# A chunked recurrence on 64x64 array tiles: wider moving operands, fewer calls, and the next chunk's systems woven into the current one

## The chip, the cores and the metric

The kernel runs on one core of a Trainium2 chip. The metric is device time in microseconds. The core's engines run their own queues side by side: TensorE (PE, matmuls and weight loads), VectorE (DVE), ScalarE (ACT), GpSimd (POOL) and SyncE (SP, whose queue issues most DMAs). They wait for one another by semaphores.

## The reference

Two blocks follow each other. The first is a linear recurrence (RWKV-7) over 768 steps, for 4 batches of 8 heads of size 40, with a 40x40 state for each:

```
y[t]  = r[t] @ state
Sa    = state @ a[t]
state = state * w[t] - outer(Sa, b[t]) + outer(v[t], k[t])
```

Its output is brought to 3072 rows of 320. The second block is a mixture of 8 experts: logits `x @ w_gate`, the best expert of each row, its softmax weight, then `relu(x @ w1[e]) @ w2[e]` (320 to 1024 to 320) times that weight, for the rows of each expert. All is in float32.

## The kernel before, in words

**The recurrence** is done in 12 chunks of 64 steps (NS). 32 sequences (batch x head) are held as two units s, each of 16 sequences: two batches with four pairs of heads make eight groups g, and the two heads of a pair (par) stand in the partitions 0 to 63 and 64 to 127. The list HD runs over the 16 pairs (g, par), so nearly every step of a unit is 16 small matmuls, one for each sequence. `eh` picks the own half of the partitions, `dh` the other one, and `qd` a quarter of 32.

Within a chunk, `decay` makes running products of w by a scan (L247), their reciprocals (L254), and scales k, a and b by them on POOL (L257). `natural` turns k, v and b from (feature, step) to (step, feature) by a matmul with a unit matrix. `gram` makes the 64x64 Gram matrices GT (k with a) and AT (v with r), masked on POOL (L296). `invert` inverts the 64x64 unit-triangular matrix of a with b: `inv_n` makes the two 32x32 diagonal blocks N and the block below them, `inv_sq` squares N four times, `inv_tt` builds the product of (I + N^k), all on 32x32 tiles of the PE array (`quads`: 32 matmuls for a unit), and `inv_w` and `inv_f` couple the two halves. `right` makes the right sides q from the state and from GT with v; `solve` multiplies by the inverse F, once as u and once turned as uT; `zgram` makes ZT; `state` the next state; `turned` its transpose; `y_state` and `y_rest` the output y; `emit` turns y to rows, adds the logits and writes rows to DRAM (x_rows).

**The order.** On PE the order is the one that is written out (`manual_schedule`); `turns` takes two calls at a time from each of its lists. In chunk c the written order is: loads of chunk c + 2 (`load_kab`), right sides with natural k and b of chunk c + 1, y from the state with GT of c + 1 and the solve, zgram with state, decay of c + 2, the rest of y with AT and natural v of c + 1, loads of v and r of c + 2, emit, and then the whole inversion for chunk c + 1, with nothing beside it but the two units' turns. On the other engines and on SP's queue a planner sets the order, by the written order and by what it takes to be ready. Buffers: kab has three for each unit, wp two, and PSUM has six banks for results of one bank and one pair of banks for y and emit.

**After the recurrence** come the routing (counts and places of the rows, in vector operations) and the experts: gathers of rows by indirect DMA, `turn`, `layer1` (L769), `layer2` (L782), and a scatter (L788). All matmuls of the recurrence are recorded under one line, L208, that of the helper `mm`; they are told apart by their tiles.

Of the kernel before, what the change touches and what calls it, by code (L numbers as in the profile page):

```python
# [8 lines left out]
F32 = mybir.dt.float32  # L9
# [12 lines left out]
def kernel(  # L22
# [16 lines left out]
    nc = tc.nc  # L39
# [79 lines left out]
    with tc.tile_pool(name="ring", bufs=1) as ring, \  # L119
         tc.tile_pool(name="sb", bufs=2) as sb, \  # L120
# [11 lines left out]
        def eh(par, n=D):  # L132
            return slice(par * 64, par * 64 + n)

        def dh(par, n=D):
            return slice((1 - par) * 64, (1 - par) * 64 + n)

        def qd(par, i):
            q = 2 * (1 - par) + i
            return slice(q * 32, q * 32 + 32)  # L140

        kab_r = [[ring.tile([128, 2, 3, NP, T2], F32, name=f"kab{s}_{i}") for i in range(3)] for s in range(NB2)]
        wp_r = [[ring.tile([128, G, T2 + 1], F32, name=f"wp{s}_{i}") for i in range(2)] for s in range(NB2)]
        x_r = [ring.tile([128, G, 64], F32, name=f"xt{s}") for s in range(NB2)]
        for tl in kab_r:
            for t in tl:
                for lo in (32, 96):
                    nc.gpsimd.memset(t[lo : lo + 32], 0.0)
        for tl in wp_r:
            for t in tl:  # L150
                for lo in (32, 96):
                    nc.gpsimd.memset(t[lo : lo + 32], 1.0)
                nc.gpsimd.memset(t[:, :, 0:1], 0.0)
# [3 lines left out]


        def padded(name, n):
            ts = [ring.tile([128, G, 64], F32, name=f"{name}{i}") for i in range(n)]  # L160
            for t in ts:
                nc.gpsimd.memset(t[:, :, D:], 0.0)
            return ts

        nk_r = [padded(f"nK{s}_", 2) for s in range(NB2)]
        st_r = [padded(f"ST{s}_", 2) for s in range(NB2)]
        s_r = [padded(f"S{s}_", 2) for s in range(NB2)]
        q_r = padded("q", NB2)


        i32 = ring.tile([128, 32], F32, name="i32")
        low32 = ring.tile([128, 32], F32, name="low32")
        for q in range(4):
            qs = slice(q * 32, q * 32 + 32)
            nc.gpsimd.tensor_copy(i32[qs], ident[qs, qs])
            nc.gpsimd.tensor_scalar(low32[qs], after[qs, qs], scalar1=-1.0, scalar2=None, op0=ALU.mult)
        up64 = ring.tile([128, T2], F32, name="up64")
        for q in range(2):
            qs = slice(q * 64, q * 64 + 64)
            nc.gpsimd.tensor_copy(up64[qs], before[qs, qs])  # L180
        for t in x_r:
            nc.gpsimd.memset(t[:], 0.0)
            for q in (0, 2):
                qs = slice(q * 32, q * 32 + 32)
                nc.gpsimd.tensor_copy(t[qs, :, 0:32], i32[qs, None, :].to_broadcast([32, G, 32]))
        iw = ring.tile([128, NP, D + E], F32, name="iw")
        for par in range(2):
            nc.gpsimd.tensor_copy(
                iw[eh(par), :, :D], ident[eh(par), None, par * 64 : par * 64 + D].to_broadcast([D, NP, D]),
            )  # L190
            nc.sync.dma_start(
                iw[eh(par), :, D:], moe_w_gate.rearrange("(p a e) x -> a e p x", p=NP, a=2)[par],
            )

        def bank(name, w=T2):
            return pp.tile([128, G, w], F32, name=name, tag="ps", bufs=6)

        def turns(*lists):

            lists = [list(l) for l in lists if l]  # L200
            while any(lists):
                for l in lists:
                    for _ in range(2):
                        if l:
                            l.pop(0)()
# [4 lines left out]
        units, wide = {}, {}  # L210

        def src(u, b2):
            c, s = u
            return c * T2 // C, c * T2 % C, 2 * s + b2

        def load_kab(u):
            c, s = u
            d = units[u] = {"kab": kab_r[s][c % 3], "wp": wp_r[s][c % 2]}
            for b2 in range(2):
                ch, o, b = src(u, b2)  # L220
                for par in range(2):
                    nc.sync.dma_start(
                        d["wp"][eh(par), b2 * NP : b2 * NP + NP, 1:], packed[b, ch, par, :, W, :, o : o + T2],
                    )
                for par in range(2):
                    nc.sync.dma_start(d["kab"][eh(par), b2], packed[b, ch, par, :, K : B_ + 1, :, o : o + T2])

        def load_vr(u):
            c, s = u
            d = units[u]  # L230
            d["vr"] = sb.tile([128, 2, 2, NP, T2], F32, name=f"vr{s}")
            for b2 in range(2):
                ch, o, b = src(u, b2)
                for par in range(2):
                    nc.sync.dma_start(d["vr"][dh(par), b2], packed[b, ch, par, :, V : R + 1, :, o : o + T2])

        def kab(d, n, g):
            return d["kab"][:, g // NP, n, g % NP, :]

        def vr(d, n, g):  # L240
            return d["vr"][:, g // NP, n, g % NP, :]

        def decay(u):
# [7 lines left out]
            wi = sb.tile([128, 2, NP, T2], F32, name="wi")  # L251
            P4 = PT[:].rearrange("q (b p) t -> q b p t", b=2)
            for h in range(2):
                nc.vector.reciprocal(wi[:, h], P4[:, h, :, 1:])  # L254
            k = d["kab"]
            for n, m in ((0, wi[:]), (1, P4[:, :, :, :T2]), (2, wi[:])):
                nc.gpsimd.tensor_tensor(k[:, :, n], k[:, :, n], m, op=ALU.mult)  # L257

        def natural(u, nm):

            c, s = u
            d = units[u]
            ps = bank("ps_nat", D)
            ts = []
            for g, par in HD:
                if nm == "V":
                    x, h, at = vr(d, 0, g), dh(par), (1 - par) * 64
                else:
                    x, h, at = kab(d, 0 if nm == "K" else 2, g), eh(par), par * 64
                ts.append(lambda x=x, h=h, at=at, g=g, par=par: mm(ps[eh(par, 64), g, :], x[h], ident[h, at : at + D]))  # L270

            def end():
                if nm == "K":
                    t = d["nK"] = nk_r[s][c % 2]
                else:
                    t = d["n" + nm] = sb.tile([128, G, D], F32, name=f"n{nm}{s}")
                nc.scalar.copy(t[:, :, :D], ps[:])
            return ts, end

        def gram(u, nm):  # L280
# [3 lines left out]
            ps = bank("ps_" + nm)  # L284
            ts = []
            for g, par in HD:
                if nm == "GT":
                    l, r, h = kab(d, 0, g), kab(d, 1, g), eh(par)
                else:
                    l, r, h = vr(d, 0, g), vr(d, 1, g), dh(par)  # L290
                ts.append(lambda l=l, r=r, h=h, g=g, par=par: mm(ps[eh(par, 64), g, :], l[h], r[h]))

            def end():
                t = d[nm] = sb.tile([128, G, T2], F32, name=f"{nm}{s}")
                nc.scalar.copy(t[:], ps[:])  # L295
                nc.gpsimd.tensor_tensor(t[:], t[:], up64[:, None, :].to_broadcast([128, G, T2]), op=ALU.mult)  # L296
# [4 lines left out]
        def quads(f):  # L301
            for g in range(G):
                for i in range(2):
                    for par in range(2):
                        f(g, par, i)

        def inv_n(u):
            c, s = u
            d = units[u]
            ps = bank("ps_N")  # L310

            def one(g, par, i):
                a, b = kab(d, 1, g), kab(d, 2, g)
                h = eh(par)
                if i == 0:
                    mm(ps[qd(par, 0), g, 32:], a[h, :32], b[h, :32])
                else:
                    mm(ps[qd(par, 1), g, :], a[h, 32:], b[h, :])
            quads(one)
            N = d["N"] = sb.tile([128, G, 32], F32, name=f"N{s}", bufs=3)  # L320
            nc.vector.tensor_tensor(N[:], ps[:, :, 32:], low32[:, None, :].to_broadcast([128, G, 32]), op=ALU.mult)
            NT = d["NT"] = sb.tile([128, G, 32], F32, name=f"NT{s}", bufs=3)
            nc.vector.transpose(NT[:].rearrange("q g t -> q (g t)"), N[:].rearrange("q g t -> q (g t)"))
            n21 = d["n21"] = sb.tile([128, G, 32], F32, name=f"n21{s}", bufs=1)
            for q in (1, 3):
                qs = slice(q * 32, q * 32 + 32)
                nc.scalar.activation(n21[qs], ps[qs, :, :32], AF.Copy, scale=-1.0)
# [537 lines left out]
```

## Time and profile before

| | |
|---|---|
| median of 3 runs | 1310.56 us (1308.91 to 1318.55) |
| the profiled execution | 1320.06 us |
| its span, first to last instruction | 1318.3 us |
| mean granted TensorE clock | 0.749 of full speed |
| PE busy / weight loads busy | 947.3 us / 735.6 us |
| DVE / ACT / POOL busy | 337.6 / 222.8 / 286.3 us |
| matmul instructions | 30652, and as many weight loads |

The profile is one execution. Busy times are unions over an engine's instructions, so a matmul's own duration (its pipeline included) is longer than the distance between two of them. "Issue" is time in which an engine waited for nothing that the profile shows. The granted clock is 1.00 for 2.4 GHz and 0.50 for 1.2 GHz.

### The profile page before, as it was taken

Reading aid. Unit: us, or ns where it says so; the run is one execution under the profiler, and the core shown is the slowest. Engines: PE = TensorE matmul, PEld = TensorE weight load, DVE = VectorE, ACT = ScalarE, POOL = GpSimd, SP = SyncE. Lnnn points to the kernel's source line nnn. Section 1 sums busy time; section 2 is a strip of 40 time slices with the busy share of each in tenths; the row PEclk is TensorE's granted clock in tenths of the full one; section 3 lists DMA queues with packets and bytes.
Section 4 is the critical chain, followed back from the end, with each engine's and each line's share of the span. In section 5 each row is a group of like instructions: output and inputs, shape, how many; then the busy total and the mean of one; then the engine's idle time right before and its main releaser. Section 6 shows DMA issues by size and latency. Waiting matters only on the chain.

```text
span 1318.3 us, 64132 instructions
## 1 busy us (share of the span) xinstructions
PE 947.3 (72%) x30652; PEld 735.6 (56%) x30652; DVE 337.6 (26%) x627; ACT 222.8 (17%) x496; POOL 286.3 (22%) x302
## 2 busy tenths in 40 slices
PE   0656575857568575866757475756479999999996
PEld 0556575746567575766757475656325544554454
DVE  1542333151514214051514212031511110111100
ACT  0212121212212121211212121211001111111110
POOL 9813231030403113030403101010132012211011
PEclk9998575665756576575757566575779999999998
DMA  3402021201102020111102010000533132322100
GB/s 67 106 4 63 11 59 29 56 22 36 43 13 52 18 59 19 36 43 31 37 5 59 9 29 9 9 10 9 130 101 114 55 100 76 115 75 89 47 15 16
DMA packets 116827, 61.86 MB, mean 47 GB/s; under 512 B 100945, under 2 KB 112211, under 8 KB 116564
## 3 DMA queue, kind: packets, MB, share of 16 engines
q1 hardware_dynamic: 110356, 48.52, 14.3%
q0 software_dynamic: 3072, 9.20, 2.3%
q8 instruction: 241, 3.95, 1.3%
q10 hardware_dynamic: 3136, 0.01, 0.1%
q14 instruction: 22, 0.18, 0.0%
HBM read 49.83 MB, written 9.19 MB: 45 GB/s over the span
## 4 chain that ended last, share of the span: by engine, by line
issue 43%; PE 39%; POOL 9%; DVE 5%; DMA 1%; SPq 1%; ACT 0%; POOLq 0%; ACTq 0%; DVEq 0%
PE ps_tt L208 7%; PE ps_sq L208 7%; PE ps_nat L208 4%; PE ps_f L208 3%; PE ps_y L208 3%; PE ps_q L208 3%; DVE wi L254 3%; POOL out_dram L788 2%; PE ps_s L208 2%; POOL xg L750 2%; PE ps_w L208 2%; PE ps_u L208 1%; POOL kab L257 1%; PE ps_GT L208 1%; DVE PT L247 1%
## 5 line engine op out<-in xcount | busy, mean ns | idle before, releaser
L769 PE MATMUL hp<-xgT,w 128*128 128x512 f32 (+1 forms) x384 | 192.0, 630 | 0.0
L208 PE MATMUL ps_tt<-TT,N 32*32 32x32 f32 x6144 | 105.8, 236 | 88.5 <-issue 84.4
L208 PE MATMUL ps_sq<-N,NT 32*32 32x32 f32 x6144 | 104.6, 236 | 87.9 <-issue 73.3
L208 PEld LDWEIGHTS ps_tt<-TT,N 32*32 32x32 f32 x6144 | 94.9, 151 | 95.3 <-issue 90.7
L208 PEld LDWEIGHTS ps_sq<-N,NT 32*32 32x32 f32 x6144 | 94.5, 151 | 95.6 <-issue 95.5
L782 PE MATMUL zp<-w,h_sb 128*128 128x320 f32 x512 | 145.0, 433 | 0.0
L769 PEld LDWEIGHTS hp<-xgT,w 128*128 128x128 f32 (+1 forms) x384 | 63.3, 189 | 123.3 <-issue 122.2
L296 POOL TENSOR_TENSOR GT<-GT,up 128x512 f32<-128x512 f32 x24 | 30.5, 1271 | 447.5 <-ACT GT L295 447.5
L208 PE MATMUL ps_nat<-ident,kab 40*64 40x40 f32 x1536 | 85.1, 295 | 44.8 <-POOL kab L257 41.8
L782 PEld LDWEIGHTS zp<-w,h_sb 128*128 128x128 f32 x512 | 94.6, 191 | 34.5 <-issue 0.8
L208 PEld LDWEIGHTS ps_nat<-ident,kab 40*64 40x64 f32 x1536 | 81.4, 212 | 46.6 <-POOL kab L257 41.8
L788 POOL DMA_INDIRECT out_dram<-zo,s_idx x32 | 31.8, 995 | 278.4 <-ACT zo L787 278.4
L774 DVE TENSOR_SCALAR h_sb<-hp 128x512 f32<-128x512 f32 x32 | 22.2, 692 | 247.1 <-PE hp L769 244.4
L254 DVE RECIPROCAL wi<-PT 128x256 f32<-128x256 f32 x48 | 82.1, 1733 | 5.3 <-POOL kab L257 3.9
L350 DVE TENSOR_TENSOR TT<-ps_tt,TT 128x256 f32<-128x256 f32 x96 | 40.8, 425 | 161.2 <-PE ps_tt L208 158.8
L338 ACT COPY N<-ps_sq 128x256 f32<-128x256 f32 x96 | 35.7, 372 | 263.5 <-PE ps_sq L208 260.6
L257 POOL TENSOR_TENSOR kab<-kab,wi 128x512 f32<-128x512 f32 x48 | 65.7, 1381 | 33.3 <-DVE wi L254 33.3
L445 DVE TENSOR_TENSOR ZT<-ps_z,up 128x512 f32<-128x512 f32 x24 | 16.6, 690 | 197.1 <-PE ps_z L208 197.1
L296 POOL TENSOR_TENSOR AT<-AT,up 128x512 f32<-128x512 f32 x24 | 41.9, 1747 | 108.5 <-ACT AT L295 108.5
L341 DVE STREAM_TRANSPOSE NT<-N 128x256 f32<-128x256 f32 x72 | 32.0, 444 | 100.1 <-ACT N L338 100.0
L776 ACT ACTIVATE h_sb<-hp 128x512 f32<-128x512 f32 x32 | 19.1, 597 | 202.9 <-PE hp L769 202.9
L208 PE MATMUL ps_f<-xt,i 32*32 32x64 f32 x768 | 45.5, 305 | 7.4 <-issue 7.4
(168 smaller groups left out, 1771.5 us busy)
## 6 DMA issues: line engine op xcount, KB each, us to landing
kab<-in_packed_dram SPq DMA_DIRECT2D x96, 120.0 KB
w<-in_moe_w_dram SPq DMA_DIRECT2D x8, 1280.0 KB
w<-in_moe_w_dram SPq DMA_DIRECT2D x8, 1024.0 KB
vr<-in_packed_dram SPq DMA_DIRECT2D x96, 80.0 KB
wp<-in_packed_dram SPq DMA_DIRECT2D x96, 40.0 KB
x_rows<-xr SPq DMA_DIRECT2D x48, 80.0 KB
w<-in_moe_w_dram SPq DMA_DIRECT2D x8, 256.0 KB
xg<-x_rows,g_idx POOLq DMA_INDIRECT x32
```

The source lines that it names most:

```text
L208: nc.tensor.matmul(out_, lhsT=lhs, rhs=rhs, start=start, stop=stop, skip_group_check=free)
L254: nc.vector.reciprocal(wi[:, h], P4[:, h, :, 1:])
L257: nc.gpsimd.tensor_tensor(k[:, :, n], k[:, :, n], m, op=ALU.mult)
L296: nc.gpsimd.tensor_tensor(t[:], t[:], up64[:, None, :].to_broadcast([128, G, T2]), op=ALU.mult)
L338: nc.scalar.copy(N[:], ps[:])
L341: nc.vector.transpose(NT[:].rearrange("q g t -> q (g t)"), N[:].rearrange("q g t -> q (g t)"))
L350: nc.vector.tensor_tensor(TTn[:], ps[:], TT[:], op=ALU.add)
L750: nc.gpsimd.indirect_dma_start(out=g["xg"][:, j, :], out_offset=None, in_=x_d[:, :], in_offset=bass.IndirectOffsetOnAxis(ap=g["gi"](j), ax ...
L769: nc.tensor.matmul(hp[:, :cols], lhsT=g["w"][0][:dsz, db, fb * 128 : (fb + 1) * 128], rhs=g["xT"][:dsz, db, :cols], start=(db == 0), stop= ...
L774: nc.vector.tensor_relu(g["h"][:, fb, :cols], hp[:, :cols])
L782: nc.tensor.matmul(zp[:], lhsT=g["h"][:, fb, j * 128 : (j + 1) * 128], rhs=g["w"][1][:, fb, :], start=(fb == 0), stop=(fb == FB - 1),)
L788: ins_ = nc.gpsimd.indirect_dma_start(out=out[:, :], out_offset=bass.IndirectOffsetOnAxis(ap=g["si"](j), axis=0), in_=zo[:], in_offset=Non ...
```

## The change

All matmuls of the recurrence use 64x64 tiles. The moving operand of a matmul is widened where two products share the stationary one. Tiles `ai` and `ri` hold a and r (64 columns) with a 40x40 unit matrix behind them, so that one matmul of 104 columns gives a Gram matrix and the turned operand: `gtk` gives GT and natural k, `atv` gives AT and natural v, `ntb` gives the system and natural b, and `zgram` gives ZT and u (so `solve` makes only uT). A tile `pair` holds the power N^k beside the inverse so far, so that one matmul of 128 columns squares and multiplies (`level`). The two 32x32 diagonal blocks stand in one 64x64 block-diagonal matrix. `couple` and `whole` take the place of `inv_w` and `inv_f`. The inversion of chunk c + 1 (`systems`) is no longer a stage of its own: `weave` takes two calls of the current chunk's list (`rest`, 416 calls) and then, on average, 1.23 calls of `systems` (256 calls). The helper `aside` puts the decay of chunk c + 2 behind the right sides. The loads of a, k and b, and those of v and r, are DMAs of their own; a and wp have one buffer for each unit, k and b two, v one. PSUM has four single banks and two pairs. The reciprocals come in four pieces for a unit instead of two.

```diff
+        a_r = tiles("a", 1, [128, 2, NP, T2])
+        kb_r = tiles("kb", 2, [128, 2, 2, NP, T2])
+        wp_r = tiles("wp", 1, [128, G, T2 + 1])
+        ai_r = tiles("ai", 2, [128, G, T2 + D])
+        ri_r = tiles("ri", 2, [128, G, T2 + D])
...
+        for t in sum(ai_r + ri_r, []):
+            nc.gpsimd.tensor_copy(t[:, :, T2:], i40[:, None, :].to_broadcast([128, G, D]))
...
+                for par in range(2):
+                    nc.sync.dma_start(d["a"][own(par, D), b2], src[par, :, A])
+                    for i, n in enumerate((K, B_)):
+                        nc.sync.dma_start(d["kb"][own(par, D), b2, i], src[par, :, n])
...
+                for p in range(0, NP, 2):
+                    nc.vector.reciprocal(wi[:, h, p : p + 2], P4[:, h, p : p + 2, 1:])
...
+        def gtk(u):
+            ps, at = halves("ps_gtk")
+            ts = [lambda g=g, par=par: mm(at(own(par), g), kb(d, 0, g)[own(par, D)], d["ai"][own(par, D), g, :])
+                  for g, par in HD]
...
+        def new_n(d, s, nt):
+            N = d["N"] = sb.tile([128, G, T2], F32, name=f"N{s}", bufs=2)
+            nc.vector.transpose(flat(N[:]), flat(nt))
...
+        def level(u, k):
+            ps = wide("ps_lv")
+            N, pair = d["N"], d["pair"]
...
+            elif k < 4:
+                ts = [lambda g=g, par=par: mm(
+                    ps[oth(par), g, :].rearrange("q (a t) -> q a t", a=2), N[oth(par), g, :], pair[oth(par), :, g, :])
+                    for g, par in HD]
...
+            def end():
+                new = pair if k == 0 else new_pair(d, s)
+                if k < 4:
+                    nc.scalar.copy(new[:, 0], ps[:, :, :T2])
+                    new_n(d, s, new[:, 0])
+                if k > 0:
+                    nc.vector.tensor_tensor(new[:, 1], ps[:, :, T2:], pair[:, 1], op=ALU.add)
+                if k == 4:
+                    new_n(d, s, new[:, 1])
...
+            while live:
+                live = False
+                for _ in range(2):
+                    live |= run(fa)
+                acc += 2.0 * nb_ / max(na, 1)
+                while acc >= 1.0:
+                    live |= run(fb)
+                    acc -= 1.0
...
+        def systems(us):
+            ps = [lambda u=u: ntb(u) for u in us]
+            ps += [lambda u=u, k=k: level(u, k) for k in range(5) for u in us]
+            ps += [lambda u=u: couple(u) for u in us] + [lambda u=u: whole(u) for u in us]
+            return ps, 16 * len(ps)
...
+        def rest(us, nx, ahead):
+            last = us[0][0] + 1 == NS
+            ps = [right(us)] + [aside(lambda u=u: decay(u)) for u in ahead] + [lambda u=u: gtk(u) for u in nx[:1]]
+            ps += [lambda u=u: solve(u) for u in us] + [lambda u=u: gtk(u) for u in nx[1:]]
+            ps += [lambda u=u: zgram(u) for u in us]
+            if not last:
+                ps += [state(us)]
+            ps += [yield_y(us)] + [lambda u=u: atv(u) for u in nx]
+            if not last:
+                ps += [lambda u=u: turned(u) for u in us]
+            ps += [emit(us)]
+            return ps, 16 * 26
...
+            weave(systems(pairs[0]), ([lambda u=u, f=f: f(u) for f in (gtk, atv) for u in pairs[0]], 64))
...
+                for u in ahead:
+                    load(u)
+                weave(rest(us, nx, ahead), systems(nx))
+                if c + 2 < NS:
+                    for u in pairs[c + 2]:
+                        load_vr(u)
```

## Rows read from the trace of the kernel before

**Rows 1.** The page: busy time of each engine, and the chain by engine.

```profile
PE 947.3 (72%) x30652; PEld 735.6 (56%) x30652; DVE 337.6 (26%) x627; ACT 222.8 (17%) x496; POOL 286.3 (22%) x302
...
issue 43%; PE 39%; POOL 9%; DVE 5%; DMA 1%; SPq 1%; ACT 0%; POOLq 0%; ACTq 0%; DVEq 0%
```

**Rows 2.** Busy time by stretch: length, then engines' busy us (count), PEclk, DMA share, GB/s.

```profile
95.00:913.00 818.00, 543.97 (x27280) 512.01 (x27276) 236.06 (x402) 169.68 (x394) 155.85 (x123) 0.63 0.13 31
...
935.50:1318.30 382.80, 346.97 (x1052) 169.79 (x1052) 62.26 (x179) 36.93 (x67) 68.13 (x68) 0.95 0.26 80
```

**Rows 3.** Timeline of PE inside an inversion: start, length, what, count, [idle before].

```profile
438.45 1.00 PE L208 MATMUL ps_sq<-N,NT 32*32 32x32 f32 x58 [1.57 <-issue]
439.23 0.25 PE L208 MATMUL ps_tt<-TT,N 32*32 32x32 f32 x3
439.27 0.24 PE L208 MATMUL ps_sq<-N,NT 32*32 32x32 f32 x1
439.28 1.10 PE L208 MATMUL ps_tt<-TT,N 32*32 32x32 f32 x65
441.94 1.01 PE L208 MATMUL ps_tt<-TT,N 32*32 32x32 f32 x59 [1.57 <-issue]
...
445.71 1.02 PE L208 MATMUL ps_sq<-N,NT 32*32 32x32 f32 x59 [1.85 <-issue]
```

**Rows 4.** The page's DMA queues: packets, MB, share of 16 engines.

```profile
q8 instruction: 241, 3.95, 1.3%
```

**Rows 5.** Timeline of PE in the last chunk, and in an expert's second layer.

```profile
919.13 1.91 PE L208 MATMUL ps_q<-nV,GT 64*64 64x40 f32 x32
...
920.83 1.84 PE L208 MATMUL ps_y<-vr,S 40*64 40x64 f32 x30
...
931.39 1.15 PE L208 MATMUL ps_y<-AT,nK 64*64 64x64 f32 x32 [0.79 <-DVE y L514]
...
1041.11 14.70 PE L782 MATMUL zp<-w,h_sb 128*128 128x320 f32 x54
```

**Rows 6.** Stretches of PE alone: length, busy us (count), PEclk, DMA share, GB/s.

```profile
426.50:465.20 38.70, 23.82 (x1371) 0.50 0.08 17
467.00:475.00 8.00, 7.58 (x268) 0.50 0.57 132
...
478.50:490.00 11.50, 6.33 (x383) 1.00 0.32 71
...
922.57:924.04 1.47, 1.47 (x66) 0.50 0.00 0
```

**Rows 7.** Groups by line and form: count | busy us, mean ns | idle before.

```profile
L254 DVE RECIPROCAL wi<-PT 128x256 f32<-128x256 f32 x48 | 82.1, 1733 | 5.3 <-POOL kab L257 3.9
L341 DVE STREAM_TRANSPOSE NT<-N 128x256 f32<-128x256 f32 x72 | 32.0, 444 | 100.1 <-ACT N L338 100.0
L445 DVE TENSOR_TENSOR ZT<-ps_z,up 128x512 f32<-128x512 f32 x24 | 16.6, 690 | 197.1 <-PE ps_z L208 197.1
L377 ACT COPY F<-ps_f 128x512 f32<-128x512 f32 x24 | 14.1, 586 | 43.9 <-PE ps_f L208 43.9
```

**Rows 8.** Timeline of DVE around the decay of both units.

```profile
492.05 1.24 DVE L247 TENSOR_TENSOR_SCAN PT<-wp,first 128x520 f32<-128x520 f32 x1
493.33 3.37 DVE L254 RECIPROCAL wi<-PT 128x256 f32<-128x256 f32 x2
...
501.39 1.75 DVE L254 RECIPROCAL wi<-PT 128x256 f32<-128x256 f32 x1
```

**Rows 9.** Timeline of SP's queue over one chunk: start, length of the issues, count.

```profile
483.06 3.40 SPq L235 DMA_DIRECT2D vr<-in_packed_dram  x8
...
501.56 1.09 SPq L534 DMA_DIRECT2D x_rows<-xr  x2
502.76 3.81 SPq L222 DMA_DIRECT2D wp<-in_packed_dram  x8
```

**Rows 10.** Timeline of PE: the first matmuls.

```profile
41.77 0.33 PE L208 MATMUL ps_nat<-ident,kab 40*64 40x40 f32 x2 [41.77 <-POOL kab L257]
```

More of the change, by code (lines that the diff above doesn't have):

```diff
@@ L172 @@
[L172 to L176, printed above, removed]
-        up64 = ring.tile([128, T2], F32, name="up64")
[L178 to L185, printed above, removed]
+        i40 = ring.tile([128, D], F32, name="i40")
@@ L212, in src, with parted, load @@
-        def src(u, b2):
+        seen = ring.tile([128, 1], F32, name="seen")
+        def parted(ps):
+            nc.scalar.copy(seen[64:65], ps[64:65, G - 1, 0:1])
+        units = {}
+        def load(u):
             c, s = u
[L214 to L218, printed above, removed]
+            d = units[u] = {"a": a_r[s][0], "kb": kb_r[s][c % 2], "wp": wp_r[s][0], "ai": ai_r[s][c % 2]}
@@ L308, in inv_n, with new_pair, ntb @@
+        def new_pair(d, s):
+            d["pair"] = sb.tile([128, 2, G, T2], F32, name=f"pair{s}", bufs=2)
+            return d["pair"]
+        def ntb(u):
             c, s = u
             d = units[u]
[L310 to L327, printed above, removed]
@@ L353, in inv_w, with end, whole @@
+            def end():
+                x = d["x"] = x_r[s][0]
+                for par in range(2):
+                    qs = slice(par * 64 + 32, par * 64 + 64)
+                    nc.scalar.copy(x[qs, :, :32], ps[qs, :, :32])
+            return ts, end
+        def whole(u):
             c, s = u
             d = units[u]
-            TT, n21 = d["TT"], d["n21"]
-            t11 = d["t11"] = sb.tile([128, G, 32], F32, name=f"t11{s}", bufs=1)
-            nc.vector.transpose(t11[:].rearrange("q g t -> q (g t)"), TT[:].rearrange("q g t -> q (g t)"))
@@ L379, in invert @@
[L379 to L414 removed]
+            ps = wide("ps_f")
@@ new lines, in whole, with end, none, right @@
+            ts = [lambda g=g, par=par: mm(ps[oth(par), g, :T2], d["x"][oth(par), g, :], d["pair"][oth(par), 1, g, :])
+                  for g, par in HD]
+            def end():
+                t = d["F"] = sb.tile([128, G, T2], F32, name=f"F{s}")
+                nc.scalar.copy(t[:], ps[:, :, :T2])
+            return ts, end
+        def none():
+            pass
+        def right(us):
+            for u in us:
+                c, s = u
+                d = units[u]
+                ps = bank("ps_q", D)
+                if c:
+                    yield [lambda g=g, par=par: mm(
+                        ps[oth(par), g, :], d["ai"][own(par, D), g, :T2], st_r[s][0][own(par, D), g, :D],
+                        start=(g == 0), stop=False, free=True) for g, par in HD], none
+                def end():
+                    t = d["q"] = q_r[s][0]
+                    nc.scalar.activation(t[:, :, :D], ps[:], AF.Copy, scale=-1.0)
+                yield [lambda g=g, par=par: mm(
+                    ps[oth(par), g, :], d["GT"][own(par), g, :], d["nv"][own(par), g, :],
+                    start=(c == 0), free=True) for g, par in HD], end
@@ L446, in zgram @@
[L446 to L471 removed]
+                un = d["u"] = sb.tile([128, G, D], F32, name="u", bufs=2)
@@ new lines, in weave, with flow, nested, run @@
+        def weave(one, two):
+            def flow(stream):
+                for piece in stream:
+                    ts, end = piece() if callable(piece) else piece
+                    for i, t in enumerate(ts):
+                        yield t, (end if i == len(ts) - 1 else None)
+            def nested(items):
+                for it in items:
+                    if isinstance(it, tuple) or callable(it):
+                        yield it
+                    else:
+                        yield from it
+            def run(f):
+                try:
+                    t, end = next(f)
+                except StopIteration:
+                    return False
+                t()
+                if end:
+                    end()
+                return True
+            (a, na), (b, nb_) = one, two
+            fa, fb = flow(nested(a)), flow(nested(b))
+            acc = 0.0
+            live = True
+            while live:
[6 more added lines that the diff above has]
+                    acc -= 1.0
+            while run(fb):
+                pass
@@ L599 @@
+                nx = pairs[c + 1] if c + 1 < NS else []
+                ahead = pairs[c + 2] if c + 2 < NS else []
+                for u in ahead:
+                    load(u)
+                weave(rest(us, nx, ahead), systems(nx))
                 if c + 2 < NS:
```

501 lines of the change are left out of this document (199 added, 302 removed).

## The prediction

> **What bounds the kernel now.** I read the profile from the whole to the part. The page first: TensorE (PE) is busy 72% of the span and its weight loads 56%, VectorE (DVE) 26%, the others less, and the chain that ended last is 43% "issue", time in which PE waits for nothing that the profile shows, and 39% PE [rows 1]. Then the busy time by stage [rows 2]: a prologue to 95 us, eleven like chunks from 95 to 913 us (818/11 = 74.4 us each, 27280 matmul instructions), the last chunk (22.5 us), and from 935.5 us the routing and the experts, 382.8 us, which the change doesn't touch. All that can change lies ahead of 935.5 us.
>
> What is the "issue" in the chunks? In the timeline of PE inside an inversion [rows 3] a pause of 1.6 to 1.85 us comes every 3.5 to 3.8 us, in the middle of a group of equal matmuls, where nothing new is waited for. From pause to pause there are 58 + 3 + 1 + 65 = 127 matmuls, and as many weight loads. The queue that brings instructions [rows 4] moved 3.95 MB in 241 packets: 16.4 KB each, or 254 of the 61304 PE instructions. So one packet feeds one period: PE is fed by code. Over the eleven chunks it is 27280 x 2 / 256 = 213 packets in 818 us, **3.84 us a packet**, waits for data included; the shortest periods in rows 3 are about 3.5. In the text one call is one matmul of the source; each is two matmul and two weight-load instructions (1248 calls a chunk, counted below, make 27456 matmuls in eleven chunks, and rows 2 have 27280, some records being missing).
>
> **The change, part by part.**
>
> *Instructions.* A chunk has 1248 calls before: 96 turning (natural), 64 Gram, 704 inversion, 64 right side, 96 y, 64 solve, 32 zgram, 64 state, 32 turned, 32 emit. After it has 256 in systems (16 pieces of 16) and 416 in rest (26 pieces): 672. That is 2688 instead of 4992 instructions, 10.5 packets instead of 19.5. At 3.84 us: 40.3 us, and at 3.5 us, if nothing else ever waits, 37. This is the first term; I take 40.3, since the 3.84 holds the ordinary waits of such a chunk.
>
> *What PE has to stream.* The new tiles are wider and fewer run side by side, so PE itself could become the bound. In the last chunk, where little is interleaved, 64x64 tiles show their pace [rows 5]: at half clock 32 instructions of 40 columns take (1.91 - 0.30)/15 = 0.107 us for each two (one on each half of the rows), 30 of 64 columns (1.84 - 0.31)/14 = 0.109; at full clock 32 of 64 columns (1.15 - 0.22)/15 = 0.062 with a start of 0.1 us in it, so 0.058. Up to 64 columns cost the same. Wide ones: 54 instructions of 320 columns in 14.70 us, 0.27 us each, 0.84 ns a column; so I take 0.090 us for 104 columns and 0.110 for 128. A piece of 16 calls is 16 such steps: 0.93, 1.44 and 1.76 us. Systems of one unit: one piece of 104 columns, four of 64, three of 128 = 10.4 us; rest of one unit: nine of up to 64, three of 104 and an emit that uses all four tiles (0.5) = 13.2 us. Two units: 47.3 us. But a second pair of tiles (rows of one half into columns of the other) runs beside the first: 66 instructions of ps_uT and ps_u pass in 1.47 us at half clock, four in 0.09 to 0.107 us [rows 6]. The crossed pieces of rest (right, solve, zgram, second half of state, last of y) are 12.2 us, and the weave sets straight pieces of systems beside them; I credit 10 us of that. So 37 us at full clock (32 if all overlaps, 47 if none): as long as the fetch, and it lies beside it.
>
> *The clock.* At half clock these 37 would be 74 us. Rows 6 show what PE did: half clock through the inversion of 32x32 tiles (1371 matmuls in 38.7 us) and through right side and turning with 40 columns, although PE was busy 7.58 of 8 us; full clock through zgram, state and y, 64 columns wide for the most part, although PE was busy only 6.33 of 11.5 us. The new pieces are 64 to 128 columns wide but for 160 of 672 calls, and between them no stretch of 32x32 tiles is left. I take full clock.
>
> *Copies.* A level ends with one copy on ScalarE (ACT) of 128x512, 0.59 us, a 32x32-block transpose on DVE, 0.44 us for 256 elements, so I estimate 0.71 for 512, and an add from PSUM, 0.69 us as ZT [rows 7]. With the 0.3 us of a matmul's end this is 2.3 us from the last matmul to the next level of that unit. Between them PE has the other unit's piece and the rest woven into it, (16 + 26) x 2 = 84 matmuls, 2.5 us at 3.84 us for 128. It is just covered: I take 0. If it is short by 0.5 us in each of 16 pieces, a chunk is 8 us longer; that goes into the range. DVE's sum for a chunk is 2 x (scan 1.3, reciprocals 3.5, six transposes 4.3, mask and four adds 3.5, and some 2.7 for ZT, state, y and emit, four operations like ZT) = 31 us: not the bound, but three quarters full.
>
> *The decay block.* The scan and reciprocals of the chunk after next now sit after the right sides. Before, they run on DVE as a block of about 11 us for both units [rows 8], and the inversion behind it waits. Cutting the reciprocals into four leaves their sum: 2 x (1.3 + 3.5) = 9.6 us. In that block the levels of both units stand; PE has at most two ready pieces and what is woven in, 84 to 168 matmuls or 2.5 to 4.7 us. So 5 to 7 us a chunk are uncovered, 0 if the order on DVE lets transposes in between. I take 5.
>
> *Loads.* 28 DMA issues a chunk become 52 on SP's queue: a, k and b apart, v and r apart (48), and four for x_rows. One takes 0.43 to 0.55 us [rows 9]: 24 us a chunk, hidden while SP never stands long. x_rows waits on SP for emit's copy at the end of a chunk, and what is queued behind it are v and r, then the next loads. ScalarE's copies, some 50 a chunk and most of them of half size or less (0.4 us by the same row), come to about 21 us, and GpSimd (POOL) has fewer: both are far from full.
>
> *Ends.* The first matmul waits until 41.77 us for POOL's setup and the first multiply [rows 10]; the memsets shrink, the eight fills with unit matrices come in, so I leave it at 42 to 44. The first systems have little woven in (64 calls): 8 levels x two units at 3.7 us (a piece of 1.1 plus 2.3, rounded up) = 30 us; the first chunk starts at 74 us instead of 95. The last chunk has 320 calls, 5 packets, 20 us.
>
> **Sum.** A chunk 40.3 + 5 = 45 us; span 74 + 11 x 45 + 20 + 383 = 972 us. The profiled execution took 1320.06 us for a span of 1318.3, so 974; the median of the runs shown is 0.7% below the profiled one, so **965 us** against 1310.56. In general the time is 0.993 x (479 + 11x), x being the chunk.
>
> **Rivals.**
> 1. *PE stays fed and the decay block is hidden* (reciprocals and transposes interleave): x = 37.5 to 40, 885 to 912 us. For it: the periods of 3.5 us in rows 3. Against: 3.84 is the mean over eleven chunks, and the block of rows 8 is solid. Chance 0.12.
> 2. *SP sets the pace.* wp and a have one buffer now. If SP keeps the written order, then after the last x_rows come 2.2 us of x_rows, 7 us of v and r and 12 us until the second unit's wp: 21 us into the chunk, while DVE reaches the scan at 6 us and stands before its transposes. x = 45 + 12 or 13, about 1100 us. For it: the sums of [rows 9]. Against: there the wp of both units are issued in one run of eight though the source has them between kab's, so the planner already moves loads to where they are free. Chance 0.14.
> 3. *The pauses belong to the levels, not to code.* Then they stay: 16 pieces x 1.7 us on top of 37, x = 64, 1175 us. Against: rows 3 have them in mid-group. Chance 0.06. The Trainium skill (Runtime: NRT & Kernel Launch, Instruction fetch mechanics) says that crossing a 16 KB boundary costs little and is mostly hidden; by that rule halving the instructions would bring nothing by itself and this rival would hold. The trace disagrees: 1.6 to 1.85 us of pause per packet.
> 4. *Half clock throughout (the slow side).* If the wide pieces, with waits between them, leave PE at 1.2 GHz as the inversion does now, a chunk is 74 us of streaming plus 5 to 8 us of waits, x = 80, the prologue 85 and the end 30: about 1370 us. It decides from x = 76 on. For it: 0.50 in [rows 6] with PE busy 95%. Against: 64 columns at less busy time had 1.00. Chance 0.06.
>
> **How the numbers follow.** The forecast (x from 41 to 50, 925 to 1020 us) has 0.62. The range 885 to 1115 takes in most of rivals 1 and 2 and the level copies that fall short; outside are rivals 3 and 4 and the tails, some 0.18. Runs here differ by 0.7%, so 1% is about what can be told from no change. Slower by over 1% is rival 4 for the most part, 0.05; within 1% a mixed clock that happens to cancel, 0.02; faster 0.93.
>
> **What would show it.** Right: about 16,000 fewer matmul instructions in the page's PE count, some 125 packets fewer on the instruction queue; chunk starts 43 to 48 us apart; PEclk 9 or 1.0 in most slices ahead of the experts; pauses without a named releaser still there but shorter, and the longest named waits of PE on DVE's N beside wi. Wrong: PEclk near 5 (rival 4); DVE's PT waiting for the wp DMA (rival 2); PE waiting for ACT or DVE at each level (rival 3, or the copies). What would break the forecast most easily is the clock: it doubles the largest term that the packets now cover.

## The result and the profile after

The changed kernel takes **950.1 us** (median of 4 runs, 949.33 to 952.1) against 1314.55 us of the kernel before, run beside it (1308.91 to 1319.39): a ratio of 0.723, 95% interval 0.719 to 0.727. The forecast was 965 us, in a range of 885 to 1115. The profiled execution took 950.85 us, its span 949.0.

The page of the kernel after: busy time and count of each engine, the granted clock in 40 slices (tenths), the instruction queue, the chain by engine. They answer to [rows 1, 4].

```profile
PE 847.2 (89%) x16828; PEld 659.7 (70%) x16828; DVE 404.0 (43%) x711; ACT 261.1 (28%) x686; POOL 281.4 (30%) x299
...
PEclk9998999999999999999999995799999999999998
...
q8 instruction: 133, 2.18, 1.0%
...
PE 38%; issue 35%; POOL 10%; DVE 8%; DMA 3%; ACT 3%; SPq 1%; POOLq 0%; DVEq 0%; ACTq 0%
```

PE has 13824 matmuls fewer, the instruction queue 108 packets fewer (241 to 133), and the granted clock is 1.00 (2.4 GHz) in every chunk but chunk 0, which has 0.93. The chain still puts 35% down to "issue", but the next view shows PE busy 97% of the steady chunks, so that share is no idle time of PE there.

Stretches of the kernel after: length, then busy us (count) of PE, PEld, DVE, ACT and POOL, PEclk, DMA share, GB/s. In order: chunk 0, chunk 1, chunk 2, the eight chunks 3 to 10, the last chunk, routing and experts. They answer to [rows 2].

```profile
74.40:124.10 49.70, 39.61 (x1224) 39.05 (x1222) 28.72 (x45) 19.65 (x54) 19.77 (x16) 0.93 0.25 56
124.10:170.80 46.70, 42.08 (x1351) 40.86 (x1347) 32.56 (x48) 18.57 (x51) 17.40 (x14) 1.00 0.31 69
170.80:214.60 43.80, 41.60 (x1355) 40.67 (x1350) 32.23 (x50) 18.67 (x52) 16.82 (x13) 1.00 0.31 70
214.60:552.80 338.20, 329.54 (x10764) 323.95 (x10759) 212.79 (x340) 148.73 (x417) 113.91 (x88) 1.00 0.22 48
552.80:569.60 16.80, 16.32 (x525) 15.75 (x519) 3.71 (x9) 4.86 (x13) 0.00 (x0) 1.00 0.11 23
569.60:949.00 379.40, 346.45 (x1020) 169.37 (x1020) 62.42 (x179) 36.77 (x66) 67.98 (x68) 0.95 0.26 81
```

A chunk took 74.4 us before; now the eight steady ones take 338.2/8 = **42.3 us** each, and PE is busy 97% of them (66% before). The waits of PE in that stretch (what it waited for: us in total, times, longest) hold only 7.1 us on named engines and some 1.4 us of "issue", which was 1.6 to 1.85 us every 3.5 to 3.8 us in [rows 3]:

```profile
PE ps_y L208 <- DVE N L309: 4.0, 10, 0.6
PE ps_lv L208 <- DVE N L309: 1.9, 8, 0.2
PE ps_lv L208 <- DVE pair L359: 1.2, 7, 0.2
```

The first three chunks are longer than the others, by 7.4, 4.4 and 1.5 us; the longest waits of PE in them are 6.1 us in all on DVE's `pair` and 4.4 us, once, on POOL's `kb`. The time that is gone is 11 x 74.4 - (552.8 - 74.4) = 340 us from the eleven chunks, 20.6 us from the start of the first chunk (95.0 to 74.4), 5.7 us from the last chunk, and 3.4 us from what follows it.

### The profile page after: what moved, and what is told of

The parts are those of the page before. It is cut to its first block, busy times and chain, and to the rows that moved or that the text cites. A ratio compares the mean times of both kernels' runs of the same rounds, so it can differ in the third digit from the quotient of the medians.

```text
span 949.0 us, 37272 instructions
## 1 busy us (share of the span) xinstructions
PE 847.2 (89%) x16828; PEld 659.7 (70%) x16828; DVE 404.0 (43%) x711; ACT 261.1 (28%) x686; POOL 281.4 (30%) x299
## 4 chain that ended last, share of the span: by engine, by line
PE 38%; issue 35%; POOL 10%; DVE 8%; DMA 3%; ACT 3%; SPq 1%; POOLq 0%; DVEq 0%; ACTq 0%
PE ps_lv L208 12%; PE ps_y L208 6%; POOL out_dram L799 3%; PE ps_ntb L208 3%; PE ps_q L208 3%; POOL xg L761 2%; PE ps_s L208 2%; PE ps_x L208 2%; PE ps_atv L208 2%; PE ps_f L208 2%; PE ps_gtk L208 2%; DVE N L309 2%; DVE pair L359 2%; PE ps_S L208 2%; DVE wi L258 2%
## 5 line engine op out<-in xcount | busy, mean ns | idle before, releaser
L208 PE MATMUL ps_lv<-pair,N 64*64 64x128 f32 (+1 forms) x3840 | 292.8, 256 | 13.2 <-DVE pair L359 8.4
L208 PEld LDWEIGHTS ps_lv<-pair,N 64*64 64x64 f32 x3840 | 249.6, 135 | 18.3 <-issue 12.6
L309 DVE STREAM_TRANSPOSE N<-pair 128x512 f32<-128x512 f32 x144 | 101.5, 705 | 96.8 <-ACT pair L356 95.5
L208 PE MATMUL ps_ntb<-ai,kb 40*64 40x104 f32 x768 | 73.4, 279 | 45.7 <-POOL kb L260 45.7
L208 PEld LDWEIGHTS ps_ntb<-ai,kb 40*64 40x64 f32 x768 | 61.4, 146 | 46.1 <-POOL kb L260 46.1
L258 DVE RECIPROCAL wi<-PT 128x128 f32<-128x128 f32 x96 | 81.6, 907 | 0.6
L260 POOL TENSOR_TENSOR kb<-kb,wi 128x512 f32<-128x512 f32 x48 | 65.9, 1390 | 26.8 <-DVE wi L258 24.5
L208 PE MATMUL ps_y<-N,off 64*64 64x64 f32 x768 | 63.4, 223 | 5.8 <-DVE N L309 5.7
L208 PE MATMUL ps_gtk<-ai,kb 40*64 40x104 f32 x768 | 68.2, 260 | 0.2 <-issue 0.2
L359 DVE TENSOR_TENSOR pair<-ps_lv,pair 128x512 f32<-128x512 f32 x96 | 63.2, 659 | 8.2 <-PE ps_lv L208 7.3
```

The source lines that it names most:

```text
L208: nc.tensor.matmul(out_, lhsT=lhs, rhs=rhs, start=start, stop=stop, skip_group_check=free)
L258: nc.vector.reciprocal(wi[:, h, p : p + 2], P4[:, h, p : p + 2, 1:])
L260: nc.gpsimd.tensor_tensor(d["kb"][:, :, i], d["kb"][:, :, i], wi[:], op=ALU.mult)
L309: nc.vector.transpose(flat(N[:]), flat(nt))
L359: nc.vector.tensor_tensor(new[:, 1], ps[:, :, T2:], pair[:, 1], op=ALU.add)
```

## The experiments

All ratios are to the kernel before, run on the same chip in the same series. "Code" is the theory of the prediction (PE is fed in packets of 256 instructions, and a packet takes 3.8 us); "streaming" is the rival that PE's own tiles set the pace; "levels" that the pauses belong to the inversion's levels.

**Wide calls cut in two** (e2): the same products, 896 calls a chunk instead of 672, still woven.

```diff
-  mm(at(own(par), g), kb(d, 0, g)[own(par, D)], d["ai"][own(par, D), g, :])
+  mm(at(own(par), g)[:, x], kb(d, 0, g)[own(par, D)], d["ai"][own(par, D), g, x])   for x in PARTS
...  # so in atv, ntb, zgram and levels 1 to 3
```

> The changed kernel with every wide call cut in two (104 into 64 and 40, 128 into 64 and 64): 896 calls a chunk instead of 672, still woven. F: 14 packets x 3.84 us = 53.8 us a chunk, 11 us more, about 1070 us (1020 at 3.5 us a packet). S: the streaming grows by 4 us a chunk, about 995 us.

Measured: 1074.6 us (1070.4 to 1078.8), ratio 0.814 [0.809, 0.818]. The stretch of its eight steady chunks, and the waits of PE in it:

```profile
252.20:679.80 427.60, 365.75 (x14348) 355.32 (x14343) 219.22 (x340) 152.70 (x416) 113.38 (x87) 0.99 0.18 39
```

```profile
PE ps_lv L210 <- issue: 21.4, 24, 1.9
PE ps_z L210 <- issue: 9.3, 7, 1.8
...
PE ps_lv L210 <- ACT nb L334: 2.7, 6, 0.5
```

```profile
q8 instruction: 175, 2.87, 1.2%
```

53.5 us a chunk, 427.6 x 128/14348 = 3.81 us for 128 matmuls and their weight loads, and the pauses without a releaser are back, in pieces of nearly every kind. Code predicted this to within 5 us. The waits on the levels' copies are as small as in the changed kernel (7.2 us in eight chunks), and the instruction queue moved 175 packets instead of 133. A price for each single instruction would give the same sums; but the pauses come in lumps: between 318.7 and 333.5 us, those of over 0.3 us lie 124, 128 and 259 recorded matmuls apart, one packet or two. The gain of the change is thus in its count of instructions.

**Half of the inversion left out of the kernel before** (e5).

```diff
+        GI = G // 2
-            for g in range(G):
+            for g in range(GI):
...
-            nc.scalar.copy(t[:], ps[:])
+            for h in range(2):
+                nc.scalar.copy(t[:, h * GI : h * GI + GI], ps[:, :GI])
```

> The kernel before, with the inversion done for half of the groups only and that half copied twice (it leaves out the other half's inverses). A chunk has 896 calls instead of 1248, the number of levels, of copies and of waits is unchanged. Code theory: 896 calls are 14 packets at 3.84 us = 54 us a chunk, about 1080 to 1100 us in all. Levels theory (the pauses belong to the levels, which stay as many; only the matmuls themselves get fewer): about 63 us a chunk, 1180 to 1200 us.

Measured: 1069.42 us (one run). Its eleven chunks:

```profile
77.10:667.00 589.90, 430.22 (x19587) 400.91 (x19588) 208.13 (x406) 155.44 (x419) 144.57 (x126) 0.68 0.18 41
```

53.6 us a chunk, 589.9 x 128/19587 = 3.86 us a packet. The number of levels is what it was and the chunk fell by 20.8 us for 352 calls less. 352 calls are 5.5 packets, 21.1 us by the code theory. The edit also halves the width of the levels' copies, which the expectation overlooked: with their transposes and adds they are busy some 4 us a chunk less, over all engines. Taken off the 63 us of the levels theory, that leaves 59, still 5 us too many, and the whole kernel is 110 us or more below what it said. The levels theory falls.

**Levels 1 to 3 narrowed** (e1): they multiply the power alone, 64 columns instead of 128, and leave the inverse's product out.

```diff
-  mm(ps[oth(par), g, :]..., N[oth(par), g, :], pair[oth(par), :, g, :])
+  mm(ps[oth(par), g, :T2], N[oth(par), g, :], pair[oth(par), 0, g, :])
```

> The changed kernel with the three 128-column levels narrowed to 64 columns: same number of calls, the product of the inverse with the power is left out there (the add reads the power's columns instead). Theory F (the code packets still set the pace, as the prediction had it): nothing changes, 940 to 950 us. Rival S (PE's own streaming sets it): 3 x 2 pieces fall from 1.76 to 0.93 us, 5 us less a chunk, 895 to 900 us.

Measured: 947.57 us (945.97 to 949.17), ratio 0.717 [0.715, 0.720]. Its eight steady chunks, and PE's waits in them:

```profile
220.10:548.40 328.30, 308.40 (x10763) 298.63 (x10760) 212.68 (x342) 149.00 (x417) 114.68 (x89) 1.00 0.23 51
```

```profile
PE ps_y L208 <- issue: 4.8, 6, 1.2
PE ps_lv L208 <- issue: 4.1, 7, 1.2
```

Code said no change, streaming 5 us less a chunk; it is 1.3 us less. PE has 21.1 us less to do in eight chunks, and 9.9 us of it arrive: 41.0 us a chunk, 3.90 us a packet, and pauses of up to 1.2 us without a releaser stand where PE was streaming. (Its first two chunks ran partly at the lower clock, 0.75 and 0.86, and took 10 us longer than those of the changed kernel, so the whole kernel gains little.) So the changed kernel's 42.3 us, set by streaming, stand just above a floor of code at 40 to 41.

**The weave taken apart** (e3): the chunk's rest first, its systems behind it.

```diff
+            if apart:
+                while run(fa):
+                    pass
-                weave(rest(us, nx, ahead), systems(nx))
+                weave(rest(us, nx, ahead), systems(nx), apart=True)
```

> The changed kernel with the systems of the next chunk run whole behind the current chunk's calls, not woven in. F alone: the packets are the same, 950 to 970 us. If waits between levels count as well: 8 steps x 3.7 us = 30 us for the systems and 23 to 26 us for the rest, 53 to 56 us a chunk, 1070 to 1100 us.

Measured: 1059.72 us (1059.5 to 1059.95), ratio 0.802 [0.800, 0.805]. Its eight steady chunks, and PE's named waits in them:

```profile
230.10:663.10 433.00, 401.87 (x10760) 389.27 (x10758) 212.78 (x340) 156.27 (x416) 112.49 (x86) 0.94 0.17 38
```

```profile
PE ps_lv L208 <- DVE pair L359: 14.2, 32, 0.6
PE ps_lv L208 <- ACT nb L332: 10.1, 8, 2.6
PE ps_y L208 <- DVE N L309: 3.8, 16, 0.3
```

54.1 us a chunk, as the theory with level waits said, but not for its reason. The named waits are 28.5/8 = 3.6 us a chunk; what grew is PE's own time, 401.87/8 = 50.2 us against 41.2 woven. One of the eight chunks was granted the full clock throughout, and a level of 64 columns in it stands alone:

```profile
557.70:609.80 52.10, 47.89 (x1352) 46.00 (x1351) 20.23 (x35) 19.46 (x52) 9.96 (x8) 1.00 0.10 22
```

```profile
602.54 1.15 PE L208 MATMUL ps_lv<-pair,N 64*64 64x64 f32 x32 [0.38 <-DVE pair L359]
```

It has 47.9 us of PE, so of the 9.0 us that PE's time grew 2.3 are the clock and 6.7 remain. These I put down to pieces that no longer run beside a crossed one: the calls are the same, and only their neighbours differ. The level alone takes 0.06 us for each two matmuls; woven with a crossed piece of y in the changed kernel, six pass in 0.11 us (lines shown under e7). **The weave mainly pairs tiles of PE**; hiding copies is its smaller part, 2.8 us of idle time a chunk.

**The weave coarser** (e4): two calls of systems at a time.

```diff
-                while acc >= 1.0:
+                while acc >= 2.0:
                     live |= run(fb)
-                    acc -= 1.0
+                    live |= run(fb)
+                    acc -= 2.0
```

> The changed kernel, the weave taking two calls of systems at a time (both halves of the rows) where it took one or two. F: no change, 945 to 955 us. S: a lone call on one half leaves the other half's tile idle; 2 to 4 us less a chunk, 905 to 930 us.

Measured: 956.2 us (951.8 to 960.5), ratio 0.723 [0.720, 0.727]. No difference, so neither theory's gain or loss shows between a grain of one or two calls and one of two; coarser grains were not run.

**No reciprocals** (e6): copies in their place.

```diff
-  nc.vector.reciprocal(wi[:, h, p : p + 2], P4[:, h, p : p + 2, 1:])
+  nc.vector.tensor_copy(wi[:, h, p : p + 2], P4[:, h, p : p + 2, 1:])
```

> The changed kernel with copies in place of the reciprocals of the decays (it leaves out the division by them). By the prediction's term, 5 us of the decay block uncovered in every chunk: 55 us off, 895 us. By the trace of the changed kernel, where DVE's block shows up as waits of PE only in the prologue and the first two or three chunks: 5 to 20 us off, 930 to 945 us.

Measured: 950.25 us (946.61 to 962.06), ratio 0.727 [0.721, 0.733]. No gain in the time, though the profiled span is 4 us shorter: less than either theory said. Its eight steady chunks, and DVE's group in them, in the changed kernel and here:

```profile
210.40:548.90 338.50, 330.19 (x10761) 324.55 (x10756) 200.80 (x340) 148.97 (x416) 113.44 (x88) 1.00 0.22 48
```

```profile
L258 DVE RECIPROCAL wi<-PT 128x128 f32<-128x128 f32 x48 | 40.4, 904 | 0.2
```

```profile
L258 DVE COPY wi<-PT 128x128 f32<-128x128 f32 x48 | 25.8, 599 | 0.2
```

A copy takes 0.60 us where a reciprocal took 0.90, so the edit shortens the block of both units by 2.4 us and doesn't take it away; the 55 us of the expectation could not have come of it. What it does show: 14.6 us less of DVE's block in the steady chunks bring nothing, they are 0.04 us longer each. So no end of the block is uncovered there. Chunks 0 and 1 are 4.4 us shorter together.

**Stacked products** (e7). If code bounds, fewer calls help. For each head, natural k and b stand in one stationary operand of 128 rows, v over u and AT over ZT in the moving ones, so that the state and y need one product each where they had two: 608 calls.

```diff
-  mm(ps[own(par), g, :], d["nk"][own(par), g, :], d["nv"][own(par), g, :], start=(g == 0), stop=False)
-  mm(ps[own(par, D), g, :], d["nb"][oth(par), g, :], d["u"][oth(par), g, :], start=False)
+  mm(ps[own(par), g, :], d["X"][:, par, g, :], d["V"][:, par, g, :])
...  # y with X and Y likewise; copies split by halves of the partitions
```

> The changed kernel with two products of the state, and two of y, stacked into one of 128 rows each: 608 calls a chunk instead of 672, about 7 copies more a unit on ScalarE and two more on VectorE. Code theory: 9.5 packets instead of 10.5 at 3.84 to 4.03 us, 4 us off each of eleven chunks: 895 to 910 us. Streaming theory (PE's tiles set the pace, and a tile of 128 rows can have no crossed one beside it): 945 to 965 us. If the added copies or the shorter cover count: up to 980 us.

Measured: 1270.11 us (1264.26 to 1275.54), ratio 0.969 [0.964, 0.975]: 320 us slower than the changed kernel, far outside what either theory said. The timeline of PE where a stacked piece is woven with a level, first at the upper clock, then at the lower:

```profile
603.51 0.32 PE L210 MATMUL ps_s<-V,X 128*64 128x40 f32 x4
603.75 0.44 PE L210 MATMUL ps_lv<-pair,N 64*64 64x128 f32 x4
604.12 0.32 PE L210 MATMUL ps_s<-V,X 128*64 128x40 f32 x4
...
608.48 0.44 PE L210 MATMUL ps_s<-V,X 128*64 128x40 f32 x4
608.85 0.69 PE L210 MATMUL ps_lv<-pair,N 64*64 64x128 f32 x4
609.47 0.44 PE L210 MATMUL ps_s<-V,X 128*64 128x40 f32 x4
```

and the stretches around: the first two of the chunk and those of the woven stacked pieces and after.

```profile
573.40:586.20 12.80, 12.80 (x239) 12.80 (x239) 3.21 (x6) 4.26 (x12) 4.30 (x4) 0.50 0.23 51
586.20:606.60 20.40, 19.02 (x487) 16.72 (x484) 11.08 (x20) 10.69 (x30) 3.12 (x3) 1.00 0.24 54
606.60:626.00 19.40, 19.40 (x157) 13.00 (x156) 6.20 (x10) 0.58 (x1) 0.00 (x0) 0.50 0.02 4
626.00:647.00 21.00, 21.00 (x350) 20.53 (x349) 10.86 (x13) 7.09 (x20) 10.00 (x8) 0.50 0.13 31
```

Every change from tiles of 128 rows to tiles of 64 and back is a step in time. Four matmuls pass, then the next four wait until they are through: 8 in 0.61 us at the upper clock, 8 in 0.99 at the lower (0.82 there where y and a level of 64 columns alternate). In the changed kernel the second half of y, on tiles of 64 rows like the level it is woven with, goes through without steps (lines of its timeline at the upper clock, six matmuls in 0.11 us):

```profile
541.31 0.28 PE L208 MATMUL ps_y<-ZT,nb 64*40 64x64 f32 x4
541.37 0.27 PE L208 MATMUL ps_lv<-pair,N 64*64 64x64 f32 x2
541.42 0.28 PE L208 MATMUL ps_y<-ZT,nb 64*40 64x64 f32 x4
```

The Trainium skill (TensorEngine Tiling (Array Packing), Key Properties) says that changing the tiling mode drains TensorE; the steps agree with it. In this stretch the granted clock falls to 0.50 (1.2 GHz) and stays there over the turn of the chunk, 53 of 74 us. The chunk of 74 us comes near the 80 of rival 4 of the prediction, but from the clock and the steps together.

**Stacked, and the output rows too** (e8): both parities of heads in one product of 88 columns, 592 calls.

```diff
-  mm(ps[b2 * 64 : b2 * 64 + 64, s, p, :], units[us[s]]["y"][own(par, D), b2 * NP + p, :], iw[own(par, D), p, :])
+  mm(ps[b2 * 64 : b2 * 64 + 64, p, :], units[us[s]]["y"][:, b2 * NP + p, :], iw[:, p, :])
```

> As the run with stacked state and y, and both head parities of the output rows taken by one product of 88 columns: 592 calls a chunk, 9.25 packets. Code theory: another 1 us off each chunk against that run, 885 to 900 us. Streaming theory: as that run, within 5 us.

Measured: 1297.68 us (1279.39 to 1317.03; the two lower times are 1279.39 and 1286.55). Two pieces of 16 calls became one of 128 rows, woven in as well, and there is no gain on e7's 1270.

**Stacked, not woven** (e9; the edit is shown against e7): as e7, but the 64 calls of 128 rows run together, with no call of systems between them.

```diff
-  d["X"][:, par, g, :], d["V"][:, par, g, :]) for g, par in HD], end
+  d["X"][:, par, g, :], d["V"][:, par, g, :]) for g, par in HD], end, True
...  # a piece marked True runs through; the weave's ratio is taken from the other calls
```

> The kernel with stacked state and y (608 calls a chunk), but their 64 calls of 128 rows now run together, with no systems' call woven between them; the weave's ratio is computed from the other calls. If what made the stacked kernel slow is the change from a tile of 128 rows to one of 64 at every second to fourth matmul, there are a few changes left a chunk and the code theory's size comes back: 9.5 packets at 3.9 us and up to 3 us of levels left standing behind the block, 37 to 41 us a chunk at full clock, 885 to 935 us. If tiles of 128 rows cost that by themselves, or the added copies do: 1150 us or more.

Measured: 996.2 us (992.74 to 999.63), ratio 0.758 [0.754, 0.762]: 274 us come back by the order of the same calls alone. So it was the changes of tile, with the lower clock that came with them, and not the 128 rows nor the copies, which e9 keeps. The stacked pieces now pass without a step (timeline); the eight chunks 3 to 10 follow, and the waits of PE in them:

```profile
400.99 2.06 PE L210 MATMUL ps_s<-V,X 128*64 128x40 f32 x64
402.87 2.06 PE L210 MATMUL ps_y<-Y,X 128*64 128x64 f32 x64
```

```profile
235.10:597.10 362.00, 317.78 (x9735) 308.56 (x9730) 233.42 (x372) 183.81 (x497) 134.44 (x104) 1.00 0.20 45
```

```profile
PE ps_lv L210 <- DVE pair L359: 26.7, 32, 1.3
PE ps_lv L210 <- ACT X L332: 9.7, 8, 1.2
PE ps_y L210 <- DVE N L309: 7.8, 12, 0.9
```

It doesn't reach the expected 37 to 41 us a chunk, but 362/8 = 45.3: the levels wait 44.2/8 = 5.5 us, presumably because less is woven with them, and PE's own time is 39.7 us. Packets (9.5 x 3.85 = 36.6) no longer set the pace.

**The first fills** (e10, e11): in e10 the padding of wp, a and kb, and `first`, is filled on VectorE instead of GpSimd, wp ahead; in e11 `first` comes ahead of a and kb too, and the second chunk's kb is filled later.

```diff
-                nc.gpsimd.memset(t[lo : lo + 32], 1.0)
+                nc.vector.memset(t[lo : lo + 32], 1.0)
...  # e11
+                for lo in (32, 96):
+                    nc.gpsimd.memset(kb_r[u[1]][1][lo : lo + 32], 0.0)
```

> The changed kernel with the fills of the padding of wp, a and kb and of first on VectorE instead of GpSimd, wp's ahead. If GpSimd's queue of fills is what the first matmul waits for, it starts at 20 to 26 us instead of 34.6 and the kernel takes 936 to 943 us. If the loads set it: no change, 950 us.

> As the run with the fills on VectorE, but first and wp are filled ahead of a and kb, and the padding of the second chunk's kb is filled by GpSimd behind the first decay blocks: VectorE's fills ahead of the first scan shrink from 16 to about 4 us. If the order of the fills sets the first matmul, it starts at 16 to 20 us instead of 23.8 and the kernel takes 936 to 942 us; if the arrival of wp and kb sets it (VectorE or GpSimd then wait for a DMA), 22 us or later and no gain against 945 us.

Measured: 944.91 us (940.88 to 946.04), ratio 0.718 [0.715, 0.720], and 943.14 us (938.27 to 944.97), ratio 0.718 [0.716, 0.720]. The first matmul of the changed kernel, of e10 and of e11:

```profile
34.61 0.44 PE L208 MATMUL ps_ntb<-ai,kb 40*64 40x104 f32 x2 [34.61 <-POOL kb L260]
```

```profile
23.75 0.50 PE L208 MATMUL ps_ntb<-ai,kb 40*64 40x104 f32 x2 [23.75 <-DMA v<-in_packed_dram]
```

```profile
20.36 0.51 PE L208 MATMUL ps_ntb<-ai,kb 40*64 40x104 f32 x2 [20.36 <-DMA wp<-in_packed_dram]
```

It starts 10.9 and 14.3 us earlier; the medians are 5 and 7 us lower, the profiled spans 6.5 and 10.0 us. The rest is lost between the first matmul and chunk 3, which starts 6.7 and 10.6 us earlier; why wasn't settled. So GpSimd's fills were what the first matmul waited for; with them gone, a DMA ends last (v in e10, wp in e11). The start came as expected in e10 (20 to 26 us) and in e11 0.4 us above the range, short of the 22 us of its rival; both times lie 1 to 2 us above what was expected. e10 and e11 can't be told apart, and the intervals of their ratios overlap the changed kernel's (0.719 to 0.727).

## Why the prediction was right, point by point

**Code feeds PE: right.** 3.84 us a packet was read from the kernel before; the split kernel has 3.81, the one with half of the inversion 3.86. The count of the change was right too (672 calls for 1248 in twelve chunks are 13824 matmuls and 108 packets, as measured); the 16,000 and 125 among the signs were a slip. The Trainium skill (Runtime: NRT & Kernel Launch, Instruction fetch mechanics) says that the crossing from one block of code to the next is mostly hidden. The changed kernel agrees, where PE has 41.2/10.5 = 3.9 us of work a packet and 0.2 us of "issue" a chunk; [rows 3] and e2 (3.3 us of work a packet, pauses of up to 1.9 us) don't.

**Streaming of 37 us beside it: mis-sized.** PE is busy 41.2 us a chunk, above the 40.3 of the packets. The 47 for no overlap was right: e3's chunk at full clock has 47.9. The credit of 10 us for crossed tiles was too large: it is 6.7. So what sets the pace of the changed kernel is streaming (41.2 and 1.1 of waits), with the code's floor 1 to 2 us below (e1).

**Full clock: right in the outcome, not in its reason.** 1.00 in all steady chunks. But of the 383 matmuls in the full-clock stretch of [rows 6], called 64 columns wide for the most part, 192 are 40 columns wide (ps_s 128, ps_S 32, ps_u 32), so those rows didn't set 64 columns apart from 40. The choice was in part luck: a chunk of e7, with pieces of 40 to 128 columns as well, was granted 0.64.

**Level copies covered: right.** 7.1 us of named waits in eight chunks. The estimate of 0.71 us for a transpose of 512 stands at 0.708.

**5 us of decay block in every chunk: wrong, the step that failed.** All of PE's named waits on DVE in the steady chunks are 7.1/8 = 0.9 us a chunk, and a shorter block brings nothing (e6). DVE's timeline says why: the written order had it behind the right sides, but the planner put it where the levels are nearly done, at the end of the chunk (here 468.2 us), with the last add and the last transpose between the first scan and its reciprocals.

```profile
458.97 1.24 DVE L247 TENSOR_TENSOR_SCAN PT<-wp,first 128x520 f32<-128x520 f32 x1
...
461.93 3.35 DVE L258 RECIPROCAL wi<-PT 128x128 f32<-128x128 f32 x4
...
466.41 3.39 DVE L258 RECIPROCAL wi<-PT 128x128 f32<-128x128 f32 x4
```

The prediction used the planner's freedom against rival 2 and not here. It also held against rival 1 that the block of [rows 8] is solid. It is not: between two of its reciprocals, in the kernel before, stands DVE's first step of the next inversion.

```profile
500.99 0.41 DVE L321 TENSOR_TENSOR N<-ps_N,low 128x256 f32<-128x256 f32 x1
```

So the half of rival 1 that has the block hidden came true. Some of the block does show in chunks 0 and 1, where e6 is 4.4 us shorter.

**SP's 52 issues hidden: right.** In the steady chunks PE has no named wait on a DMA. The loads of r and v are issued late, not in one run at the head of the chunk:

```profile
450.72 5.48 SPq L241 DMA_DIRECT2D ri<-in_packed_dram  x8
461.12 5.09 SPq L240 DMA_DIRECT2D v<-in_packed_dram  x8
```

**The ends.** First chunk at 74.4 (74 said), though the first matmul came at 34.6 and not at 42 to 44: two errors cancel, which is luck. Last chunk 16.8 (20): without a next chunk it has 16 pieces, 256 calls and not 320, so 4 packets or 15.4 us. The rest 379.4 (383).

**The sum.** A chunk of 45 became 40.3 + 2.0 (streaming above code) + 0 + 1.2 (the first three chunks' 13.3 us over eleven) = 43.5: 17 us less in all. The ends took off 6.5, so the span is 949 instead of 972. The prediction went 7 us below its span, by a factor of 0.993 taken from a profiled execution that was longer than the median; this time the two agree (950.85 and 950.1), 1 us above the span. That gave 8 us back. (By that factor 974 us would have been 967, not 965.) The mechanism, code and then streaming close above it, was right; that the chunk came within 1.5 us is in part luck, since the 5 us for the decay block stood in for 2.0 of streaming and 1.2 of the first chunks that the sum didn't have. The steady chunks, 42.3 us apart, lie just outside the 43 to 48 named as a sign.

## What to carry to other kernels

Count instructions before columns: in these kernels many small matmuls waited for their code, at nearly one price a packet (3.81 to 3.90 us) whatever they computed, and a wider moving operand paid by the calls it saved until PE's own streaming was reached; beyond that point the packets no longer set the time. When two streams of matmuls are woven, keep them on one height of tile, or run the odd pieces together. Where a planner orders an engine, price a moved block by the gaps that the planner can find for it, not by its place in the source.

## What the runs showed of the hardware that was not expected

- The price of a packet of code doesn't follow PE's clock: 3.86 us at a mean granted clock of 0.68 (e5), 3.81 at 0.99 (e2).
- Alternating every four matmuls between tiles of 128 and of 64 rows took 0.3 us for each four at the upper clock and 0.5, for the same pieces, at the lower; 64 of them, all on tiles of 128 rows, pass in 2.06 us (0.13 for four). The order alone is worth 274 us here.
- In that stretch the clock fell to its lower level although PE's busy time by the profile was 19.40 of 19.40 us: that stretch, with 157 matmuls in it, had 0.50, and the one before it, with 487 in 20.40 us, had 1.00.
